# A long convolution in front of a recurrence: class sums and the skip product on GpSimd, inverses of 16 matmuls, later masks, and another way for the kernel values through DRAM

## The chip, the core and the metric

The kernel runs on one core of one Trainium2 chip. The core has five engines: TensorE (PE in the profile, with its weight loads as PEld), VectorE (DVE), ScalarE (ACT), GpSimd (POOL) and SyncE (SP). They share an on-chip memory of 128 partitions (SBUF); results of matmuls land in PSUM. Transfers run on 16 DMA engines and are issued from the queues of SP, ACT and POOL. The metric is the device time of one execution in microseconds, as the median of several runs of the same program.

## What is computed

Two independent parts are computed and concatenated along the last axis, for one batch of 2048 rows:

```python
# A: recurrent attention over segments of 32 rows, with 8 memory rows
for s in range(64):
    h = concat(mem, x[32*s : 32*s+32])            # 40 rows of 1024
    q, k, v = h @ Wq, h @ Wk, h @ Wv              # 32 heads of 128
    o = softmax(mask(q @ k.T / sqrt(128))) @ v
    o = o @ Wo                                    # 1024 wide
    mem = o[:8];  outs.append(o[8:])
# B: a long convolution, for each of 1024 columns d
K[d, l] = real(sum_n C[d,n] * exp(dt[d] * A[d,n] * l) * dt[d] * B[d,n])     # N = 128
y[l, d] = sum_{m <= l} K[d, l-m] * u[m, d]  +  u[l, d] * Dskip[d]
```

The reference does the convolution by FFT of length 4096. All inputs and the output are bf16.

## The kernel before

**Stage one** (0 to about 395 us of the profile) makes tables for part B, projections of those rows of part A that need no memory, and the kernel values K at chosen places. It is a list of steps in an order written out by hand (`ORDER`, L690), gone through 16 times (L1339). One transform of u into the frequency domain runs in it as a side job; its results, for four groups of 256 columns (`dq`) and four blocks of frequencies (`kc`), go to DRAM as `Ud` (L1011). GpSimd makes sums and differences there (L1007 to L1010, in `classes`). The values of K come out in two halves of 512 columns each, in tiles `KxT`. In `put_values` (L1072) the first half is written from SBUF into a DRAM buffer `Kd` with 44 small DMAs, each put into a list `late` that gives up one entry at each exponential (L1276). The second half is written whole as `Kx1` (L1075).

**Stage two** (about 395 to 632 us) has 16 passes, b = 0 to 15, one for each pair (dq, kc). A pass does the following.

- PE makes the spectrum of K for the next pass, `spectrum(b + 1, ...)` (L1238): 40 matmuls of 128x256 into tiles `hps` (before pass 4 `pa`), from values `ks` in SBUF.
- DVE multiplies it by the transform of u (`times_u`, L1394, four operations, one input in PSUM and one in SBUF), then turns (`rotate`, L1397 and L1398, both inputs in SBUF), then makes the sum and the difference of two halves (L1469, both inputs in SBUF) into a bf16 tile `Bt`.
- SP loads the next pass's `Ud` block (`load_u`, L1229), and weights of part A into places that have come free (`next(resident)`, L266).
- From b = 4 on, PE does two inverses (`products_back`, L1519): 32 matmuls of 128x256 each, from `Bt` of the dq before and the matrices `MI`. ACT makes negated copies of parts of `MI` for them (L1485) and writes the result as bf16 (`yb`, L1534). In the next pass DVE multiplies a loaded piece `uu` of u by `Dsk` (L1539) and adds `yb` (L1540), ACT issues the output DMA.

After pass 15 eight inverses are left, three of them begun with the first three blocks (`inverse_begin`); between them SP issues twelve weight loads and then one at a time (L1620).

Beside that, at b = 2 GpSimd multiplies four rows of values by four rows of u (L1596), and behind it in its queue, at b = 4, stand the identity and the masks of part A (`constants`, L222: 36 operations at L235 and some more). The second half's values are put in order by `load_second` (L1091): 12 small DMAs a pass from DRAM to SBUF (L1102) or to DRAM (L1105) at b = 3 to 6, and one load at the end (L1108). `spectrum(8, ...)`, which PE runs in pass 7, is the first to use them.

**Stage three** (632 us to the end) is part A: 64 segments one after the other. In each, PE goes through all weights; most stay in SBUF, twelve blocks of 512 KB are loaded again in each segment through four slots `wst` (L334). The first segment also loads the last weights of Wo (`W_o`, L266).

All queues are filled in program order (`manual_schedule`): what stands behind a waiting instruction on its engine waits too.

Of the kernel before, what the change touches and what calls it, by code (L numbers as in the profile page):

```python
# [221 lines left out]
def constants(tc, ahead):  # L222
# [4 lines left out]
    make_identity(nc, ident[:])  # L227
    nc.gpsimd.memset(mask[:], 0.0)
# [18 lines left out]
    ahead.consts = ident, mask, BD, BDx, BDL, hT  # L247
    return hT
# [454 lines left out]
def part_b(ctx, tc, u, A_re, A_im, B_re, B_im, C_re, C_im, log_dt, Dskip, out_b, ahead, copies, residents, first_state):  # L703
# [12 lines left out]
    Kd = dram.tile([641, DH], BF16, name="Kd")  # L716
    Kx1 = dram.tile([128, NF * 128], BF16, name="Kx1")
    Kd1 = dram.tile([256, DH], BF16, name="Kd1")
# [340 lines left out]
    def part_out(sb, h, kp):  # L1059
# [4 lines left out]
        if sb % 8 == 7 and h == 1:  # L1064
            put_values(sb)

    late = []

    PLACED = ((0, 0, ((8, 1, 32),)), (8, 256, ((8, 2, 16),)), (16, 384, ((4, 1, 4), (8, 4, 8), (40, 1, 4))),
              (24, 512, ((0, 1, 4), (4, 2, 2), (8, 8, 4), (40, 2, 2), (44, 1, 4))))  # L1070

    def put_values(sb):  # L1072
        kx = KxT["t"]
        if sb // 8:
            late.append(lambda: sy.dma_start(out=Kx1[:], in_=kx[:].rearrange("p j c -> p (j c)")))  # L1075
            return

        def put(out, in_):
            late.append(lambda: sy.dma_start(out=out, in_=in_))
        for g in range(4):  # L1080
            dsl = slice(128 * g, 128 * g + 128)
            for p0, u0, cols in PLACED:
                n_j = sum(n for _, _, n in cols)
                dst = Kd[u0:u0 + 8 * n_j, dsl].rearrange("(i j) d -> i j d", j=n_j)
                at = 0
                for j0, js, n in cols:
                    put(dst[:, at:at + n], kx[32 * g + p0:32 * g + p0 + 8, j0:j0 + js * (n - 1) + 1:js, :])
                    at += n
            put(Kd[640:641, dsl], kx[32 * g + 31:32 * g + 32, NF - 1, :])

    def load_second(KT):  # L1091
        rows = Kx1[:].rearrange("p (j c) -> p j c", j=NF)
        for g in range(4):
            for p0, u0, cols in PLACED:
                n_j = sum(n for _, _, n in cols)
                at, p = 0, 32 * g + p0
                for j0, js, n in cols:
                    src_ = rows[p:p + 8, j0:j0 + js * (n - 1) + 1:js, :]
                    if len(cols) == 1:
                        for lo in range(0, 8 * n_j, 128):  # L1100
                            o = DH * ((u0 + lo) // 128) + 128 * g
                            sy.dma_start(out=KT[:, o:o + 128], in_=src_[lo // n_j:(lo + 128) // n_j])  # L1102
                            yield
                    else:
                        sy.dma_start(out=Kd1[u0 - 384:u0 - 384 + 8 * n_j, 128 * g:128 * g + 128].rearrange("(i j) d -> i j d", j=n_j)[:, at:at + n], in_=src_)  # L1105
                        yield
                    at += n
        sy.dma_start(out=KT[:, 3 * DH:5 * DH].rearrange("p (j d) -> p j d", j=2), in_=Kd1[:].rearrange("(j p) d -> p j d", p=128))  # L1108

    def load_k(KT, lo):  # L1110
        n_ = KT.shape[1] // DH
        sy.dma_start(out=KT.rearrange("p (j d) -> p j d", j=n_), in_=Kd[128 * lo:128 * (lo + n_), :].rearrange("(j p) d -> p j d", p=128))
        return [KT[:, DH * j:DH * j + DH] for j in range(n_)]
# [664 lines left out]
```

## Time and profile before

| | |
|---|---|
| median of 3 runs | 1980.21 us (1974.15 to 1983.52) |
| the profiled execution | 1981.69 us, its span 1979.9 us |
| mean granted TensorE clock | 0.977 |
| PE busy | 1840.5 us (93%) |
| DVE busy | 1371.1 us (69%) |
| ACT busy | 949.7 us (48%) |
| GpSimd (POOL) busy | 389.8 us (20%) |
| moved by DMA | 589.91 MB, mean 298 GB/s |

The profile's page gives busy times, a picture of the span in 40 slices, the DMA queues, and the chain of work that ended last. The trace behind it can be asked for groups of instructions by line, for the order of time on an engine, for waits, and for busy time in given stretches. A line such as L1394 is a line of the kernel. A row of a timeline has the start, the length (both in us), the engine, the line, the operation, what it writes and reads with its shape, and how many such instructions were merged; in brackets stands the engine's idle time ahead of it and what ended it. The tile names are the program's own.

### The profile page before, as it was taken

To read this page: it belongs to the slowest core of one execution; us is meant where nothing else is said; L and a number is where in the kernel's file an instruction comes from. 1 tells how busy PE (TensorE), PEld (TensorE's weight loads), DVE (VectorE), ACT (ScalarE), POOL (GpSimd) and SP (SyncE) were. 2 spreads that over 40 slices of the span, in tenths; PEclk is the share of its full clock that TensorE was granted. 3 is DMA by queue.
4 is the path that set the end of the run, shared out by engine and by line. 5 is a ranking of instruction groups with operands and counts; after the bars stand their busy time and mean duration, and the time that the engine had idled before them with its cause. 6 is when DMAs were issued, how large, how long until landed. Compare 5 with 4: busy or idle time off the path is not lost.

```text
span 1979.9 us, 74693 instructions
## 1 busy us (share of the span) xinstructions
PE 1840.5 (93%) x32006; PEld 1133.3 (57%) x32044; DVE 1371.1 (69%) x3401; ACT 949.7 (48%) x1678; POOL 389.8 (20%) x823
## 2 busy tenths in 40 slices
PE   8999999787998799999999999999999999999999
PEld 3666566456786455555555555555555555555554
DVE  8699999787893466666666666767666666666650
ACT  8799999832123344434444444444434343434330
POOL 2354454212000111111111111111111111111120
PEclk9999999779999799999999999999999999999999
DMA  7989888765478899999999999999999999999991
GB/s 221 255 238 265 264 239 251 210 223 185 144 250 298 312 338 336 351 333 339 340 338 333 348 347 345 350 339 349 340 336 341 337 344 338 344 342 348 328 344 37
DMA packets 329728, 589.91 MB, mean 298 GB/s; under 512 B 87812, under 2 KB 203368, under 8 KB 327220
## 3 DMA queue, kind: packets, MB, share of 16 engines
q1 hardware_dynamic: 277208, 530.64, 78.4%
q10 hardware_dynamic: 45532, 29.57, 4.9%
q0 software_dynamic: 6656, 24.92, 3.4%
q8 instruction: 251, 4.11, 0.9%
q14 instruction: 81, 0.66, 0.1%
HBM read 528.52 MB, written 67.26 MB: 301 GB/s over the span
## 4 chain that ended last, share of the span: by engine, by line
PE 40%; DMA 22%; DVE 3%; ACT 1%; issue 1%; POOL 0%; ACTq 0%; SPq 0%; POOLq 0%; DVEq 0%
PE acc L408 23%; DMA wst<-WD_o 8%; PE pp L521 8%; DMA wst<-WD_v 6%; DMA wst<-WD_k 3%; PE pe L658 3%; PE tr L419 2%; DMA arena<-PKd 2%; DMA wst<-WD_q 1%; DMA out_dram<-arena 1%; PE pv L489 1%; DVE arena L615 1%; PE pv L493 1%; PE sc L433 1%; ACT arena L615 1%
## 5 line engine op out<-in xcount | busy, mean ns | idle before, releaser
L408 PEld LDWEIGHTS <-a_hT 128*32 128x32 bf16 x12352 | 328.2, 96 | 308.8 <-issue 54.0
L414 ACT CAST arena<-acc 128x512 bf16<-128x512 f32 x384 | 225.1, 586 | 395.0 <-PE acc L408 317.6
L521 PEld LDWEIGHTS <-arena 128*32 128x32 bf16 x8256 | 217.0, 96 | 91.0 <-issue 66.4
L408 PE MATMUL acc<-wst,a_hT 128*32 128x512 bf16 x2304 | 229.4, 381 | 24.1 <-DMA wst<-WD_v 16.4
L422 POOL COPY arena<-arena 128x128 bf16<-128x128 bf16 x128 | 37.3, 292 | 842.5 <-DMA arena<-PKd 274.0
L329 DVE TENSOR_SCALAR arena<-keep 128x256 int32<-128x256 int32 (+1 forms) x512 | 175.7, 395 | 31.5 <-PE acc L408 29.1
L408 PE MATMUL acc<-XM,a_hT 128*32 128x512 bf16 x2560 | 185.9, 380 | 0.0
L521 PE MATMUL pp<-W_o,arena 128*32 128x256 bf16 x3584 | 122.6, 274 | 7.3 <-DMA W_o<-in_A_Wo_dram 7.3
L452 ACT ACTIVATE sc<-sc 128x160 f32<-128x160 f32 (+1 forms) x192 | 63.9, 333 | 126.0 <-DVE sc L449 125.5
L448 DVE TENSOR_REDUCE a_mx<-sc 128x4 f32<-128x160 f32 (+1 forms) x192 | 71.7, 373 | 75.0 <-PE sc L436 75.0
L197 PE MATMUL pro<-XM,wsl 128*128 128x512 bf16 x480 | 117.4, 382 | 5.9 <-DVE kst L206 2.2
L408 PE MATMUL acc<-W,a_hT 128*32 128x512 bf16 x1536 | 119.3, 382 | 0.2 <-issue 0.2
L536 DVE COPY arena<-tr 128x512 bf16<-128x512 bf16 x64 | 27.2, 425 | 126.2 <-PE tr L419 126.2
L456 DVE TENSOR_REDUCE a_mx<-sc 128x4 f32<-128x160 f32 (+1 forms) x192 | 72.9, 379 | 55.4 <-ACT sc L452 55.0
L1519 PE MATMUL yp<-Bt,MI 128*128 128x256 bf16 x680 | 105.2, 274 | 0.0
L408 PE MATMUL acc<-g,a_hT 128*32 128x512 bf16 x1024 | 102.2, 381 | 0.0
L1283 DVE TENSOR_SCALAR nr<-ptt 128x456 f32<-128x456 int16 x128 | 80.3, 628 | 29.8 <-PE ptt L1261 26.9
L483 POOL TENSOR_TENSOR arena<-arena,a_BD 128x128 bf16<-128x128 bf16 x128 | 51.0, 399 | 237.8 <-DVE arena L466 222.8
L615 ACT CAST arena<-pp 128x128 bf16<-128x128 f32 x64 | 17.0, 266 | 164.9 <-DVE arena L615 164.9
L1275 ACT ACTIVATE E<-pa 128x648 bf16<-128x648 f32 x128 | 87.8, 713 | 15.8 <-PE pa L1267 13.9
L521 PE MATMUL pp<-wst,arena 128*32 128x256 bf16 x1536 | 76.6, 275 | 19.3 <-DMA wst<-WD_o 17.4
L408 PE MATMUL acc<-wq,a_hT 128*32 128x512 bf16 x1024 | 91.2, 382 | 0.0
(333 smaller groups left out, 4024.4 us busy)
## 6 DMA issues: line engine op xcount, KB each, us to landing
wst<-WD_v SPq DMA_DIRECT2D x256, 512.0 KB
wst<-WD_k SPq DMA_DIRECT2D x192, 512.0 KB
wst<-WD_o SPq DMA_DIRECT2D x192, 512.0 KB
wst<-WD_q SPq DMA_DIRECT2D x128, 512.0 KB
Ud<-ux POOLq DMA_DIRECT2D x16, 1024.0 KB, 8.2
wq<-Ud SPq DMA_DIRECT2D x32, 512.0 KB
wsl<-in_A_Wk_dram SPq DMA_DIRECT2D x16, 512.0 KB
wsl<-in_A_Wv_dram SPq DMA_DIRECT2D x16, 512.0 KB
```

What stands on the lines that cost most here:

```text
L197: nc.tensor.matmul(a[:], lhsT=w[:, kc, 128 * j:128 * j + 128], rhs=xTl[:, kc, :, :].rearrange("p s k -> p (s k)"), start=(kc == 0), stop=( ...
L329: nc.vector.tensor_scalar(out=out.bitcast(I32), in0=in_.bitcast(I32), scalar1=0, scalar2=None, op0=ALU.bitwise_or)
L408: nc.tensor.matmul(a[32 * g:32 * g + 32, o_:o_ + rhs.shape[1]], lhsT=hT[:, kc, :], rhs=rhs, start=(kc == 0), stop=(kc == KC - 1), tile_pos ...
L414: nc.scalar.copy(out=q, in_=a[:])
L448: nc.vector.tensor_reduce(out=m_, in_=x, axis=AX.X, op=ALU.max)
L452: nc.scalar.activation(out=flat(sc, i), in_=flat(sc, i), func=ACT.Exp, scale=scale)
L456: nc.vector.tensor_reduce(out=m_, in_=x, axis=AX.X, op=ALU.add)
L521: nc.tensor.matmul(po[32 * qt:32 * qt + 32, o_:o_ + rhs.shape[1]], lhsT=oT[:, h % 4, (h % 16) // 4, :], rhs=rhs, start=False, stop=(h == 3 ...
L658: nc.tensor.matmul(pe[n][:], lhsT=left[2 * b + hi // 16][:, 128 * (hi % 16):128 * (hi % 16) + 128], rhs=wo[u][:, 1024 * hh + 512 * n:1024 ...
L1275: sc.activation(out=T["E", r, e // 4][:, lo:lo + 8 * NE].rearrange("p (i c) -> p i c", i=2), in_=T.pop(("p", r, e))[:, :, 0:4 * NE], func= ...
L1283: v.tensor_scalar(out=T["n", r, e // 4][:, lo:lo + 8 * NT], in0=T.pop(("t", r, e))[:, 0:8 * NT].bitcast(I16)[:, 0:16 * NT:2], scalar1=floa ...
L1519: pe.matmul(yp[:, b, :], lhsT=m_[:, b, cs, kc, :], rhs=Bt[:, kc, j, half, c_, :], start=(kc == 0 and cs == 0 and half == 0), stop=(kc == 3 ...
```

## The change

- The sum and the difference of the two halves (L1469) go to an f32 tile `halves_` (one buffer) instead of `Bt`. GpSimd then makes the second sums in four operations of 128x512, two of them with the order of cosine and sine parts turned round, and writes bf16 `Bt` with eight parts a block.
- An inverse therefore has 16 matmuls instead of 32, and no negated copies of `MI`.
- `Dsk` is multiplied once by PLEN/2 on GpSimd (in stage one, at f = 10). GpSimd multiplies each loaded `uu` by it right behind its load (`load_inverse`), and an identity matmul for each half of an inverse adds the product to PSUM. The two DVE operations L1539 and L1540 go; the output DMA reads `yb` itself. `uu` has 5 buffers instead of 7, `yb` 4 instead of 2.
- `constants` makes only the identity at b = 4; the masks follow behind the sixth of the last eight inverses.
- Each half of the kernel values is written whole to DRAM by four DMAs (`Kx`, 256 bytes a piece), eight DMAs from DRAM to DRAM put two of its five blocks in order (`Kp`), and five loads bring them to SBUF. For the first half that is in stage one; for the second the eight DMAs are issued four each at b = 3 and 4, the loads at b = 6.

The core of the diff:

```diff
 def constants(tc, ahead):
     make_identity(nc, ident[:])
+    ahead.consts = ident, mask, BD, BDx, BDL, hT
+    yield hT
     nc.gpsimd.memset(mask[:], 0.0)
 ...
     def put_values(sb):
-        kx = KxT["t"]
-        if sb // 8:
-            late.append(lambda: sy.dma_start(out=Kx1[:], in_=kx[:].rearrange("p j c -> p (j c)")))
-            return
+        kx, half = KxT["t"], sb // 8
         for g in range(4):
 ...
+            late.append(lambda g=g: sy.dma_start(out=Kx[half][:, :, g, :], in_=kx[32 * g:32 * g + 32, :, :]))
+        late.extend([lambda: None] * (16 if half == 0 else 0))
+        for p0, cols in PIECES:
+            at = 0
+            for j0, js, n in cols:
+                (late if half == 0 else second).append(lambda p0=p0, at=at, j0=j0, js=js, n=n: sy.dma_start(
+                    out=Kp[half][p0 - 16:p0 - 8, at:at + n, :],
+                    in_=Kx[half][p0:p0 + 8, j0:j0 + js * (n - 1) + 1:js].rearrange("i j g c -> i j (g c)")))
+                at += n
 ...
     for f in range(16):
+        if f == 10:
+            gp.tensor_scalar(out=Dsk[:], in0=Dsk[:], scalar1=float(PLEN / 2), scalar2=None, op0=ALU.mult)
 ...
     def pointwise(b, s_):
+        X = halves_
         for j, op in ((0, ALU.add), (1, ALU.subtract)):
-            v.tensor_tensor(out=Bt[:, kc, j], in0=Y[:, 0], in1=Y[:, 1], op=op)
+            v.tensor_tensor(out=X[:, j], in0=Y[:, 0], in1=Y[:, 1], op=op)
+        for r, op in ((0, ALU.add), (2, ALU.subtract)):
+            gp.tensor_tensor(out=Bt[:, kc, 2 * r:2 * r + 2], in0=X[:, 0, 0], in1=X[:, 0, 1], op=op)
+        gp.tensor_tensor(out=Bt[:, kc, 2:8:5], in0=X[:, 1, 0], in1=X[:, 1, 1, ::-1], op=ALU.add)
+        gp.tensor_tensor(out=Bt[:, kc, 3:7:3], in0=X[:, 1, 0, ::-1], in1=X[:, 1, 1], op=ALU.subtract)
 ...
-    NIV, UU = 3, 7
+    NIV, UU = 3, 5
     def load_inverse(dq, c):
         sy.dma_start(out=uu[:], in_=u_v[r][:, mc:mc + 2, d])
+        gp.tensor_tensor(out=uu[:], in0=uu[:], in1=Dsk[:, d].unsqueeze(1).to_broadcast([128, 2, DQ]), op=ALU.mult)
 ...
                 for cs in range(2):
-                    g_cs = cs if j == 0 else 1 - cs
-                    minus = neg is not None and neg[0] <= cs < neg[1]
-                    for half, m_, c_ in ((0, MI[c // 2], cs), (1, mn if minus else MI[c // 2], g_cs)):
-                        pe.matmul(yp[:, b, :], lhsT=m_[:, b, cs, kc, :], rhs=Bt[:, kc, j, half, c_, :], start=(kc == 0 and cs == 0 and half == 0),
-                                  stop=(kc == 3 and cs == 1 and half == 1), skip_group_check=True)
+                    pe.matmul(yp[:, b, :], lhsT=MI[c // 2][:, b, cs, kc, :], rhs=Bt[:, kc, 2 * r + cs, :], start=(b == 0 and kc == 0 and cs == 0),
+                              stop=False, skip_group_check=True)
+            if kcs[-1] == 3:
+                pe.matmul(yp[:, b, :], lhsT=ident[:], rhs=uu[:, b, :], start=False, stop=True, skip_group_check=True)
 ...
-        def ending():
-            v.tensor_tensor(out=uu[:], in0=uu[:], in1=Dsk[:, d].unsqueeze(1).to_broadcast([128, 2, DQ]), op=ALU.mult)
-            v.tensor_tensor(out=uu[:], in0=uu[:], in1=yb[:], op=ALU.add)
-            unsent.append(lambda: sc.dma_start(out=out_v[r][:, mc:mc + 2, d], in_=uu[:]))
+        unsent.append(lambda: sc.dma_start(out=out_v[r][:, mc:mc + 2, d], in_=yb[:]))
 ...
-        for _ in range(12 if 2 < b < 7 else 0):
-            next(second, None)
+        for _ in range(4 if b in (3, 4) else 0):
+            second.pop(0)()
+        if b == 6:
+            ks.append(load_k(1, k1[:, 0:2560], 0))
 ...
     for n_ in range(8):
         inverses(1)
-        end()
+        if n_ == 5:
+            next(state)
```

More of the change, by code (lines that the diff above doesn't have):

```diff
@@ L715, in part_b @@
     Ud = dram.tile([4, 4, 128, 4, 2, DQ], F32, name="Ud")
-    Kd = dram.tile([641, DH], BF16, name="Kd")
-    Kx1 = dram.tile([128, NF * 128], BF16, name="Kx1")
-    Kd1 = dram.tile([256, DH], BF16, name="Kd1")
+    Kx = [dram.tile([32, NF, 4, 128], BF16, name="Kx%d" % i) for i in range(2)]
+    Kp = [dram.tile([16, 16, DH], BF16, name="Kp%d" % i) for i in range(2)]
     MId = dram.tile([16, 128, 2, 4, 128], BF16, name="MId")
@@ L1091, in load_second @@
[L1091 to L1108, printed above, removed]
@@ new lines, in put_values, with load_k @@
+        for p0, cols in PIECES:
[5 more added lines that the diff above has]
+                at += n
+    def load_k(half, KT, lo):
+        n_ = KT.shape[1] // DH
+        ks_ = [KT[:, DH * j:DH * j + DH] for j in range(n_)]
+        for j, t_ in enumerate(ks_):
+            c = lo + j
+            src_ = Kp[half][8 * (c - 3):8 * (c - 2)] if c > 2 else Kx[half][4 * c:4 * c + 4, 8:40] if c < 2 else Kx[half][8:16, 8:40:2]
+            sy.dma_start(out=t_, in_=src_ if c > 2 else src_.rearrange("i j g c -> i j (g c)"))
+        return ks_
@@ L1493, in inverses @@
             dq, c = todo.pop(0)
-            if not ready:
-                ready.append(negated(c))
-            inverse(dq, c, nxt.pop(0), *ready.pop(0))
+            inverse(dq, c, nxt.pop(0))
             if len(todo) >= NIV:
@@ L1728, in first_state @@
         nc = tc.nc
-        hT = constants(tc, ahead)
+        consts = constants(tc, ahead)
+        hT = next(consts)
         nc.sync.dma_start(out=xt[:].rearrange("p k r -> p (k r)"), in_=ahead.VXd[0, :, 256:])
```

72 lines of the change are left out of this document (19 added, 53 removed).

## The prediction, made before the changed kernel was run

> **What bounds the kernel now.** I read the busy time by stage first. The rows have the stretch, its length, the busy time of PE, PEld, DVE, ACT and POOL with instruction counts, the granted clock, the busy share of the DMA engines, and GB/s.
>
> ```profile
> 395.00:453.00 58.00, 49.60 (x399) 33.31 (x388) 49.32 (x46) 17.61 (x36) 14.19 (x35) 0.77 0.62 215
> 453.00:518.00 65.00, 48.53 (x397) 40.21 (x395) 43.38 (x49) 11.71 (x13) 4.27 (x17) 0.87 0.58 183
> 518.00:600.00 82.00, 82.00 (x744) 71.41 (x743) 74.89 (x86) 24.39 (x27) 0.00 (x0) 1.00 0.63 196
> 600.00:672.00 72.00, 55.84 (x667) 38.10 (x665) 22.95 (x63) 21.42 (x31) 2.80 (x8) 0.90 0.94 326
> 672.00:1979.00 1307.00, 1238.72 (x25523) 715.23 (x25524) 833.29 (x2594) 519.59 (x1141) 205.53 (x513) 1.00 0.92 329
> ```
>
> The change leaves stage three (the last row) alone, and adds to stage one only work beside its matmuls. So the passes and the stretch behind them count. From 518 us PE is busy without a gap, DVE is close behind, GpSimd does nothing, and the DMA engines have a third free. From 600 us DMA is at 0.94. Between 453 and 518 us nothing is full: something waits. In the order of time, DVE:
>
> ```profile
> 429.92 2.36 DVE L1469 TENSOR_TENSOR Bt<-y 128x1024 bf16<-128x1024 f32 x2
> ...
> 451.04 2.36 DVE L1469 TENSOR_TENSOR Bt<-y 128x1024 bf16<-128x1024 f32 x2
> ...
> 515.74 2.36 DVE L1469 TENSOR_TENSOR Bt<-y 128x1024 bf16<-128x1024 f32 x2
> ...
> 565.08 1.22 DVE L1394 TENSOR_TENSOR z<-wq,hps 128x1024 f32<-128x1024 f32 x1
> 566.21 1.22 DVE L1394 TENSOR_TENSOR y<-wq,hps 128x1024 f32<-128x1024 f32 x1
> ...
> 569.60 0.42 DVE L1539 TENSOR_TENSOR uu<-uu,Dsk 128x512 bf16<-128x512 bf16 x1
> ...
> 571.67 0.42 DVE L1540 TENSOR_TENSOR uu<-uu,yb 128x512 bf16<-128x512 bf16 x1 [0.73 <-ACT yb L1534]
> 572.01 1.22 DVE L1397 TENSOR_TENSOR y<-y,z 128x1024 f32<-128x1024 f32 x1
> 573.15 1.22 DVE L1398 TENSOR_TENSOR y<-y,z 128x1024 f32<-128x1024 f32 x1
> 574.40 2.36 DVE L1469 TENSOR_TENSOR Bt<-y 128x1024 bf16<-128x1024 f32 x2
> ...
> 597.75 2.36 DVE L1469 TENSOR_TENSOR Bt<-y 128x1024 bf16<-128x1024 f32 x2
> ```
>
> The sums L1469 mark the ends of passes 2, 4, 8, 13 and 15. Passes 14 and 15 took (597.75 - 574.40) / 2 = 11.68 us each, but 5 to 8 took (515.74 - 451.04) / 4 = 16.2 us each: four passes lost 18 us. The whole stretch from 4 to 15 took 146.7 us. An operation of 128x1024 takes a slot of 1.13 us (565.08 to 566.21). The matmuls of a steady pass:
>
> ```profile
> 516.41 6.71 PE L1519 MATMUL yp<-Bt,MI 128*128 128x256 bf16 x60
> ...
> 523.71 4.53 PE L1238 MATMUL hps<-k,XM 128*128 128x256 bf16 x40
> 528.08 0.27 PE L1519 MATMUL yp<-Bt,MI 128*128 128x256 bf16 x1
> ```
>
> At 4.37 us for 40 (523.71 to 528.08, 0.109 us each) a pass is 40 + 64 matmuls and two small ones, 11.6 us: **PE sets the pass**. What slowed passes 5 to 8 is in the waits between 400 and 640 us and in SP's order:
>
> ```profile
> DVE z L1394 <- DMA wq<-Ud: 17.2, 4, 6.0
> PE hps L1238 <- DMA k<-Kd: 11.7, 1, 11.7
> ```
>
> ```profile
> 444.89 7.06 SPq L1105 DMA_DIRECT2D Kd<-Kx  x8
> ...
> 552.69 0.89 SPq L1477 DMA_DIRECT2D uu<-in_B_u_dram  x2
> ```
>
> Twelve small DMAs a pass cost SP some 0.9 us each, over 10 us, and the next `Ud` block stands behind them.
>
> **The change, part by part.**
>
> *Work that goes from PE and DVE.* An inverse has 16 + 2 matmuls instead of 32: 28 x 0.109 = 3.1 us a pass, and PE needs 8.5 us. DVE loses two pairs L1539 and L1540 and keeps eight slots, 9.1 us. The negated copies on ACT (24 us busy of 82) are off the path: nothing.
>
> *Work that GpSimd gets.* Its nearest rows:
>
> ```profile
> 26.96 3.18 POOL L916 TENSOR_TENSOR part<-x,part 128x1024 bf16<-128x1024 f32 x1 [13.63 <-ACT part L906]
> 35.25 2.13 POOL L916 TENSOR_TENSOR part<-x,part 128x1024 bf16<-128x1024 f32 x1 [5.11 <-ACT part L906]
> ...
> 136.90 1.27 POOL L1007 TENSOR_TENSOR ux<-us 128x512 f32<-128x512 f32 x1 [2.23 <-DVE us L1036]
> 138.14 1.27 POOL L1008 TENSOR_TENSOR ux<-us 128x512 f32<-128x512 f32 x1
> 139.37 2.78 POOL L1010 TENSOR_TENSOR ux<-us 128x256 f32<-128x256 f32 x4
> ...
> 437.35 2.11 POOL L1596 TENSOR_TENSOR k<-g,k 4x1024 bf16<-4x1024 bf16 x1 [64.52 <-DMA k<-in_B_u_dram]
> 440.82 1.01 POOL masks.py:199 TENSOR_SCALAR_AFFINE_SELECT a_ident<-a_ident 128x128 bf16<-128x128 bf16 x1
> 442.02 13.78 POOL L235 TENSOR_SCALAR_AFFINE_SELECT a_mask<-a_mask 32x24 bf16<-32x24 bf16 x36
> ```
>
> ```profile
> L483 POOL TENSOR_TENSOR arena<-arena,a_BDL 128x128 bf16<-128x128 bf16 x128 | 51.4, 401 | 0.0
> L886 POOL TENSOR_TENSOR x<-natAr,dtb 128x1024 f32<-128x1024 bf16 x1 | 1.9, 1892 | 6.3 <-DMA natAr<-in_B_A_re_dram 6.3
> ```
>
> A class sum of 128x512 f32: 1.24 us (136.90 to 138.14). Bounds: half of the shorter L916, 1.06, and half of the longer, 1.59. The product u times D, 128x512 bf16 with one operand repeated: half of L1596, 1.05, half of L886, 0.95, or four times L483, 1.6. I take 1.1, near the two that have long rows. A pass gives GpSimd 4 x 1.24 + 2 x 1.1 = 7.1 us. Alone this would fit beside DVE's 9.1.
>
> *But the two engines exclude each other.* On DVE, beside the GpSimd rows at 26.96 and 437.35:
>
> ```profile
> 26.94 1.22 DVE L892 SCALAR_TENSOR_TENSOR x<-y,y 128x1024 f32<-128x1024 f32 x1
> ...
> 436.51 1.22 DVE L1394 TENSOR_TENSOR y<-wq,pa 128x1024 f32<-128x1024 f32 x1
> 437.76 2.78 DVE L1397 TENSOR_TENSOR y<-y,z 128x1024 f32<-128x1024 f32 x1
> ```
>
> L1397 has two SBUF inputs; it took 2.78 instead of 1.22 us, and ended 1.1 us after the GpSimd product (437.35 + 2.11 = 439.46). L1394, one input in PSUM, overlapped the same product and kept its 1.22 us. On the other side, the first L916 began behind L892, which has two SBUF inputs, and was 1.05 us longer than the second. So of DVE's eight slots the last four (L1397, L1398, two L1469) cannot run beside GpSimd, the four L1394 can. A pass then is 4.94 (class sums, beside 4 x 1.13 of L1394) + 4 x 1.13 + 2 x 1.1 = 11.7 us; behind the product L1397 needed 1.08 us instead of 1.22, so at a pass's three turns from GpSimd to DVE I take 0.3 off: **11.4 us, about what PE's 11.68 is now**. The bound has changed, and the steady pass hardly gains. PE has room: even at the first row's clock of 0.77 it would need 8.5 / 0.77 = 11.0 us. Bounds, all rows low or high: 10.2 (0.2 more for hand-overs) and 4.54 + 5.2 (two sums in two pieces of 0.69, as L1010) + 3.2 = 13.0.
>
> The Trainium skill says this too (SBUF — State Buffer, section "SBUF: two separate sides"): a DVE operation with two SBUF inputs and a GpSimd operation that reads SBUF take one port pair in turns, each for its whole length. That rule speaks against moving the sums; the trace agrees, with 2.78 against 1.22 us. It has no gain at the hand-over and would give 11.7 us a pass and 1965 us in the end. The skill's GPSIMD Engine Reference (3.1 Elementwise) gives 2.6 cycles an element at 1.2 GHz, by which a 128x512 operation is an estimated 1.1 us, the class sum too: 0.5 us less a pass and about 1956 us in the end.
>
> *The second half's values.* The 48 small DMAs become four at b = 3, four at b = 4 and five at b = 6. At 0.9 us each SP is held 3.6 to 4.5 us in these passes, less than the 6.7 us (four slots, two products) between the last L1394 of a pass, which frees the `Ud` tile, and the first of the next. The 17.2 and 11.7 us of waits go, and passes 5 to 8 run at the steady length: 11 passes at 11.4, and 1.2 us for the identity between them, 126.6 instead of 146.7: **20.1 us gained** (bounds 33 and 3).
>
> *b = 2 to 4.* In GpSimd's queue stand the class sums of pass 2, L1596 with three small followers (437.35 to 440.82, 3.4 us), three products (3.3), and only then the class sums of pass 3, which pass 4's sums on DVE need (one buffer). From the end of pass 2 (432.3) these are 4.9 + 3.4 + 3.3 + 4.9 us, with four turns of DVE for pass 3 between them (4.5) and three to four for pass 4 behind (4.0): 25.0 us to the end of pass 4, against 453.4 - 432.3 = 21.1 now. **4 us lost** (bounds 3 and 6). If a row piece or a `uu` lands late, GpSimd waits at the head of its queue, the sums behind it, then DVE. From b = 4 on there is room: pass 11 ends at 576.8 - 2 x 11.68 = 553.4, its `uu` loads are issued at 552.69, and 4.9 us of class sums stand ahead of their products.
>
> *The four dumps in place of `Kx1`, the 12 DMAs in place of 44 in stage one, `Dsk` times a constant.* Nothing: the first half's blocks are wanted only in the last of stage one's sixteen rounds, some five rounds after they are written; the second half's dumps stand on SP ahead of pass 2's `Ud` block, where DMA is at 0.62 and GpSimd busy 14 of 58 us. Without that cover up to 5 us, one block late by a dump or two.
>
> *The tail and the masks.* The chain that ended last has:
>
> ```profile
> 652.67 6.94 DMA W_o<-in_A_Wo_dram
> ...
> 659.67 11.44 DMA wst<-WD_o
> ```
>
> Behind pass 15 the eight inverses need half the matmuls, some 12 us less. But DMA is at 0.94 there, the last `uu` loads stand behind twelve weight loads, and weights set the end of the first segment. PE cannot pass them. I take **3 us gained** (bounds 6 gained, 2 lost). The masks (13.8 us) now run behind the last products, while segment one starts; the scores that want them stand in the middle of a segment of 1307 / 63 = 20.7 us, so they may be 3 us late, in front of the longer waits for weights: nothing. If no such wait is left, 3 us.
>
> **The sum**: -20.1 + 4 - 3 = -19.1. The profiled execution took 1981.7 us (1979.9 span, 1.8 around it), 1.5 above the median, 1980.2. From the one 1962.6, from the other 1961.1: **1962 us**.
>
> **The rivals.**
> - *The engines run side by side*: then DVE's 9.2 us bound the pass: 11 x 9.2 = 101, 45.5 gained, with the tail and nothing lost at b = 3 about 49: 1932 us. For it: L1394 was not slowed. Against: L1397 was. 8%.
> - *GpSimd is dearer, and the passes get longer*: with 1.59 a sum and 1.6 a product a pass is 4.54 + 6.36 + 3.2 = 14.1, eleven 155 + 1: 9.6 lost instead of 20.1 gained, 7 at b = 3, 1 gained behind: 1997 us. It decides from a pass of 13.1 us, that is 8.6 to 8.9 of GpSimd's time. For it: the turned order and the repeated operand stand in no f32 row. Against: L1007, L1008. 13%.
> - *The passes gain, the end does not*: if transfers alone set the first segment's end, only the tail changes: 1979 us. For it 0.94 of DMA from 600 us. Against: these loads wait for places that the passes free, and at 518 to 600 us a third is free. 9%.
>
> **How the numbers follow.** The forecast has 70%; its own range is 1946 to 1985 by the bounds of its terms. It takes in the third rival and leaves out the first and the second, 21%, of which the second's lower end lies within; so the range is 1946 to 1985. Half a per cent (10 us) is about what a measurement can tell from no change. Of the forecast's 70% I give 62 to faster by more than that, 7 to within, 1 to slower; the first rival is faster, the second slower, the third within: faster 0.70, same 0.16, slower 0.14.
>
> **What would show it.** Steps: L1394 and L1238 wait no more for `Ud` and values between 453 and 518 us; passes of 11.4 us with PE no longer full; L1397, L1398 and the sums stretched to 2 us or more wherever GpSimd works, L1394 not; class sums at 1.24, products at 1.1; the first segment's wait for `WD_o` still there. Wrong if DVE keeps 1.22 us throughout (first rival) or GpSimd's operations alone are over 1.5 us (second).

## The result

The changed kernel takes 1965.28 us (median of 13 runs, 1962.06 to 1978.45); beside it on the same chip the kernel before took 1979.36 us (13 runs). The ratio is 0.9949, with a 95% interval of 0.9924 to 0.9974. The profiled execution took 1964.7 us (span 1962.9), 17.0 less than the one before. The forecast was 1962.

In the busy time by stage (the columns are those of the table of before) PE is no longer full in the passes, and the slow stretch from 453 us is gone:

```profile
453.00:518.00 65.00, 54.03 (x453) 44.24 (x451) 64.17 (x46) 7.16 (x12) 58.23 (x37) 0.92 0.67 212
518.00:590.00 72.00, 58.24 (x468) 46.87 (x467) 65.79 (x49) 7.76 (x13) 65.91 (x42) 0.91 0.75 231
```

DVE and GpSimd (the third and the fifth busy time) are both busy for nine tenths or more from 453 to 590 us. How they share a pass stands in the order of time, first DVE, then GpSimd. The line numbers are those of the changed kernel: L1374 is the multiplication (before L1394), L1377 and L1378 the rotation, L1451 the pair of half sums (before L1469), L1453 to L1455 the class sums, L1465 the product of u and D.

```profile
457.67 3.24 DVE L1451 TENSOR_TENSOR hv<-y 128x1024 f32<-128x1024 f32 x2
...
514.00 3.12 DVE L1451 TENSOR_TENSOR hv<-y 128x1024 f32<-128x1024 f32 x2
...
562.11 1.21 DVE L1374 TENSOR_TENSOR z<-wq,hps 128x1024 f32<-128x1024 f32 x1
...
565.50 1.21 DVE L1374 TENSOR_TENSOR y<-wq,hps 128x1024 f32<-128x1024 f32 x1
...
568.01 2.17 DVE L1378 TENSOR_TENSOR y<-y,z 128x1024 f32<-128x1024 f32 x1
570.28 3.12 DVE L1451 TENSOR_TENSOR hv<-y 128x1024 f32<-128x1024 f32 x2
...
581.50 3.12 DVE L1451 TENSOR_TENSOR hv<-y 128x1024 f32<-128x1024 f32 x2
```

```profile
561.13 3.41 POOL L1453 TENSOR_TENSOR Bt<-hv 128x512 bf16<-128x512 f32 x2 [1.16 <-DVE hv L1451]
...
565.74 1.27 POOL L1455 TENSOR_TENSOR Bt<-hv 128x512 bf16<-128x512 f32 x1
566.97 4.22 POOL L1465 TENSOR_TENSOR uu<-uu,Dsk 128x512 bf16<-128x512 bf16 x2
```

From pass 9 to pass 15 a pass took (581.50 - 514.00) / 6 = 11.25 us on average (single ones 10.4 to 12.2), against a forecast of 11.4. The four L1374 ran beside the class sums and kept 1.21 us. L1378, with two SBUF inputs, began beside the first product and took 2.17; the pair L1451 took 3.12 in place of 2.36. From pass 4 to 15 it is 123.8 us (457.67 to 581.50) in place of 146.7.

The first segment still ends with the wait for a weight, and its first transposition of a new state (`tro`, the first sign of a finished segment, here "the first state") came 16.6 us earlier; pieces of the chain of work, first of the kernel before, then of the changed one:

```profile
672.63 0.59 PE tro L621 x2
```

```profile
642.77 11.74 DMA wst<-WD_o
...
656.02 0.58 PE tro L622 x2
```

The 17.0 us by stretches of the two profiled executions, against the forecast's terms:

| stretch | forecast | measured |
|---|---|---|
| up to the sums of pass 0 (402.4, now 406.2) | 0 | +3.8 |
| sums of pass 0 to those of pass 4 (48.6, now 51.5) | +4 | +2.9 |
| pass 4 to pass 15 (146.7, now 123.8) | -20.1 | -22.9 |
| the pair of sums of pass 15 (2.4, now 3.1) | 0 | +0.7 |
| its end to the first state (72.5, now 71.4) | -3 | -1.1 |
| first state to the end (1307.3, now 1306.9) | 0 | -0.4 |
| sum | -19.1 | -17.0 |

### The profile page after: what moved, and what is told of

The parts are those of the page before. It is cut to its first block, busy times and chain, and to the rows that moved or that the text cites. A ratio compares the mean times of both kernels' runs of the same rounds, so it can differ in the third digit from the quotient of the medians.

```text
span 1962.9 us, 73759 instructions
## 1 busy us (share of the span) xinstructions
PE 1799.1 (92%) x31558; PEld 1089.2 (55%) x31596; DVE 1370.2 (70%) x3337; ACT 918.9 (47%) x1654; POOL 543.4 (28%) x920
## 4 chain that ended last, share of the span: by engine, by line
PE 45%; DMA 28%; DVE 18%; ACT 6%; issue 4%; POOL 0%; SPq 0%; ACTq 0%; DVEq 0%; POOLq 0%
PE acc L409 22%; DMA wst<-WD_v 9%; DMA wst<-WD_o 9%; PE pp L522 8%; DMA wst<-WD_k 3%; PE pe L659 3%; DMA wst<-WD_q 2%; PE tr L420 2%; DMA arena<-PKd 2%; PE pro L184 2%; DVE nr L1261 2%; DVE y L1374 1%; DVE hv L1451 1%; PE pa L1216 1%; DVE y L1378 1%
## 5 line engine op out<-in xcount | busy, mean ns | idle before, releaser
L409 PE MATMUL acc<-W,a_hT 128*32 128x512 bf16 x1536 | 119.2, 381 | 0.0
L1504 ACT ACTIVATE yb<-yp 128x512 bf16<-128x512 f32 x29 | 17.3, 597 | 157.9 <-PE yp L1492 146.4
L522 PE MATMUL pp<-wst,arena 128*32 128x256 bf16 x1536 | 76.5, 275 | 15.4 <-DMA wst<-WD_o 13.1
```

The costliest lines, as they stand in the source:

```text
L409: nc.tensor.matmul(a[32 * g:32 * g + 32, o_:o_ + rhs.shape[1]], lhsT=hT[:, kc, :], rhs=rhs, start=(kc == 0), stop=(kc == KC - 1), tile_pos ...
L522: nc.tensor.matmul(po[32 * qt:32 * qt + 32, o_:o_ + rhs.shape[1]], lhsT=oT[:, h % 4, (h % 16) // 4, :], rhs=rhs, start=False, stop=(h == 3 ...
```

## The experiments

The theory is the prediction's: SP's queue of small DMAs held passes 5 to 8, which is where the gain lies; elsewhere PE's bound gave way to one as long, DVE and GpSimd taking turns. The rivals: the gain came with the halved matmuls and the work on GpSimd; or a pass is bound by something else (PE's lower clock, GpSimd's whole time).

Times of one kernel spread over 10 us and more, so mechanisms are read from stretches of the profiles: from the pair of sums in pass 4 to that in pass 15, and from the end of the latter to the first state. Each stretch is that of one execution. Ratios are to the kernel before on the same chip, with 95% intervals; the runs used several chips, so medians of different rows are compared through the ratios.

| kernel | median us | ratio | pass 4 to 15 | 15 to first state |
|---|---|---|---|---|
| before | 1979.4 | 1 | 146.7 | 72.5 |
| changed | 1965.3 | 0.9949 [0.9924, 0.9974] | 123.8 | 71.4 |
| values_alone | 1962.8 | 0.9941 [0.9918, 0.9963] | 126.9 | 69.5 |
| sums_alone | 1976.7 | 1.0002 [0.9976, 1.0029] | 140.0 | 70.0 |
| product_dve | 1960.4 | 0.9932 [0.9910, 0.9954] | 122.7 | 69.9 |
| dsk_late | 1966.8 | 0.9968 [0.9944, 0.9991] | 124.9 | 72.8 |
| no_class_sums | 1947.4 | 0.9844 [0.9809, 0.9879] | 115.8 | 74.5 |
| masks_early | 1975.2 | 0.9991 [0.9971, 1.0011] | 132.7 | 72.2 |
| tail_loads_first | 1977.5 | 1.0010 [0.9990, 1.0029] | 125.5 | 76.5 |
| turns_fewer | 1960.0 | 0.9913 [0.9881, 0.9945] | 119.3 | 71.2 |
| stores_at_once | 1968.5 | 0.9963 [0.9944, 0.9981] | 125.4 | 72.6 |
| turns_fewer_2 | 1953.0 | 0.9886 [0.9857, 0.9916] | 119.2 | 69.8 |
| stores_by_gpsimd | 1978.5 | 1.0008 [0.9989, 1.0028] | 122.1 | 85.1 |
| dumps_spread | 1965.4 | 0.9942 [0.9917, 0.9967] | 126.8 | 71.1 |

### The two halves of the change, each alone

`values_alone` is the kernel before with the new `put_values`, `load_k` and `second` alone:

```diff
-    Kd = ...; Kx1 = ...; Kd1 = ...
+    Kx = [dram.tile([32, NF, 4, 128], BF16, ...) for i in range(2)]
+    Kp = [dram.tile([16, 16, DH], BF16, ...) for i in range(2)]
...
-        for _ in range(12 if 2 < b < 7 else 0):
-            next(second, None)
+        for _ in range(4 if b in (3, 4) else 0):
+            second.pop(0)()
+        if b == 6:
+            ks.append(load_k(1, k1[:, 0:2560], 0))
```

> The kernel before with the new way of the kernel values alone (four dumps a half, pieces, block loads); sums, inverses, products and masks as before. Theory (SP's queue of small DMAs held passes 5 to 8, PE sets all others): passes 5 to 8 fall from 16.2 to 11.7 us each, the stretch from pass 4 to pass 15 from 146.7 to about 130 us, and the time falls by 16 to 17 us, to about 1963: nearly the whole gain of the change. If the dumps also cost the first stage something, its rounds 9 and 10 (18.7 us each in the kernel before) get longer here. Rival (the gain came with the sums, products and half the matmuls): the time stays above 1974 and passes 5 to 8 stay above 14 us.

`sums_alone` is the changed kernel with these hunks undone.

> The changed kernel with the kernel values moved the old way (44 small stores, one dump of the second half, 48 small loads in passes 3 to 6); sums, inverses of 16, products on GpSimd, identity and late masks stay. Theory: passes 5 to 8 wait for SP again, some 16 us each; the seven other passes are 0.5 us shorter than PE's 11.7, 3.4 us gained in all, against 3.6 us lost at passes 2 to 4 and 3 us in the first stage: 1978 to 1984 us, no faster than before. Rival (the gain came with this part): 1970 us or less.

DVE's pairs of sums, first in `values_alone` (passes 4, 8 and 15), then in `sums_alone` (pass 8; there the pair of pass 4 began at 456.92); below them DVE's wait for `Ud`, first in `values_alone` between 453 and 518 us, then in `sums_alone` between 453 and 530 us:

```profile
455.79 2.36 DVE L1446 TENSOR_TENSOR Bt<-y 128x1024 bf16<-128x1024 f32 x2
...
500.78 2.36 DVE L1446 TENSOR_TENSOR Bt<-y 128x1024 bf16<-128x1024 f32 x2
...
582.65 2.36 DVE L1446 TENSOR_TENSOR Bt<-y 128x1024 bf16<-128x1024 f32 x2
```

```profile
518.89 2.36 DVE L1474 TENSOR_TENSOR hv<-y 128x1024 f32<-128x1024 f32 x2
```

```profile
DVE z L1371 <- DMA wq<-Ud: 0.8, 1, 0.8
```

```profile
DVE z L1397 <- DMA wq<-Ud: 19.4, 4, 7.3
```

With the values alone passes 5 to 8 take 11.2 us each; with the sums alone (518.89 - 456.92) / 4 = 15.5, and the wait for `Ud` is as long as in the kernel before. The one half carries the whole gain, the other none: the theory holds, the first rival falls. By the medians `values_alone` gained 10.6 us on its chip (1962.8 against 1973.4), less than the 16 to 17 expected. The sums alone do shorten the stretch from pass 4 to 15 by 6.7 us, but passes 0 to 4 took 3.4 us longer in that trace and began 2.5 us later, and the time did not move.

### What makes a steady pass

`product_dve` gives the products back to DVE; the identity matmul stays.

```diff
-        gp.tensor_tensor(out=uu[:], in0=uu[:], in1=Dsk[:, d]..., op=ALU.mult)
+        unmade.append(lambda: v.tensor_tensor(out=uu[:], in0=uu[:], in1=Dsk[:, d]..., op=ALU.mult))
...
         next(points)
+        products()          # runs what stands in unmade; also ahead of each last inverse
```

> The changed kernel with the products of u and D on DVE, as in the kernel before (0.42 us each), instead of on GpSimd; the identity matmul still adds them. Theory of turns (a pass is the class sums beside the four L1374, then the four DVE operations with two SBUF inputs and the products, one at a time): a pass is 4.94 + 4.53 + 2 x 0.42 - 0.2 = 10.1 us instead of 11.2; 12 us less in eleven passes, 2 to 3 us less at passes 2 to 4 and behind the last: 1949 to 1952 us. Rival 1 (PE at the lower granted clock, or the single buffer of the half sums, sets the pass): passes stay at 11.2 us and the time within 3 us of the changed kernel. Rival 2 (weights set the end): passes fall to 10.1, the time does not.

DVE in one pass of it, and GpSimd beside it:

```profile
506.38 2.36 DVE L1451 TENSOR_TENSOR hv<-y 128x1024 f32<-128x1024 f32 x2
...
513.19 1.01 DVE L1469 TENSOR_TENSOR uu<-uu,Dsk 128x512 bf16<-128x512 bf16 x2
514.12 1.21 DVE L1377 TENSOR_TENSOR y<-y,z 128x1024 f32<-128x1024 f32 x1
...
516.57 1.23 DVE L1451 TENSOR_TENSOR hv<-y 128x1024 f32<-128x1024 f32 x1
```

```profile
507.75 3.36 POOL L1453 TENSOR_TENSOR Bt<-hv 128x512 bf16<-128x512 f32 x2 [4.36 <-DVE hv L1451]
...
512.29 1.28 POOL L1455 TENSOR_TENSOR Bt<-hv 128x512 bf16<-128x512 f32 x1
```

DVE has more to do than in the changed kernel, and yet the pass is 516.57 - 506.38 = 10.2 us, as expected (10.1): nothing is stretched any more but the products themselves, which begin before the last class sum ends. The time is not shown to be below that of the changed kernel (the intervals overlap; 1949 to 1952 us was expected), since passes 5 and 7 took 14.8 and 13.9 us. In both DVE stood before a product whose `uu` was late on SP, in pass 7 behind the five loads of values, in pass 5 behind four pieces, of whose 10.05 us 7.4 were a wait for a store of ACT (more on that below):

```profile
468.55 0.43 DVE L1469 TENSOR_TENSOR uu<-uu,Dsk 128x512 bf16<-128x512 bf16 x1 [4.35 <-DMA uu<-in_B_u_dram]
```

```profile
455.24 10.05 SPq L1079 DMA_DIRECT2D Kp<-Kx  x4
```

`no_class_sums` leaves the class sums out; DVE's pair writes what the matmuls read.

```diff
-            v.tensor_tensor(out=X[:, j], in0=Y[:, 0], in1=Y[:, 1], op=op)
-        for r, op in ...: gp.tensor_tensor(out=Bt[...], ...)
-        ...
+            v.tensor_tensor(out=Bt[:, kc, 4 * j:4 * j + 4]..., in0=Y[:, 0], in1=Y[:, 1], op=op)
```

> The changed kernel without the class sums: DVE's pair writes what the matmuls read, and GpSimd keeps the products alone (what the matmuls read is then not the class sums). Theory of turns (the class sums run beside the four L1374 and cost nothing; the four DVE operations with two SBUF inputs and the two products go one at a time): a pass is 4.53 + 4.53 + 2.2 - 0.2 = 11.0 to 11.1 us against 11.2 with the class sums, though GpSimd has 4.9 us less to do; a few us are gained at passes 2 to 4. Rival (GpSimd's whole time, or the loop through the one buffer of half sums, makes the pass): a pass falls to DVE's 9.1 to 9.3 us and pass 15 ends 20 us earlier.

Passes of 9.3 to 11.3 us came out from pass 8 on. GpSimd's products, then DVE, in one of the shortest and in the longest:

```profile
517.49 2.27 POOL L1460 TENSOR_TENSOR uu<-uu,Dsk 128x512 bf16<-128x512 bf16 x2 [7.96 <-PE hps L1216]
...
554.16 4.24 POOL L1460 TENSOR_TENSOR uu<-uu,Dsk 128x512 bf16<-128x512 bf16 x2 [6.99 <-DMA uu<-in_B_u_dram]
561.04 3.25 POOL L1460 TENSOR_TENSOR uu<-uu,Dsk 128x512 bf16<-128x512 bf16 x2 [2.63 <-DMA uu<-in_B_u_dram]
```

```profile
514.35 2.36 DVE L1450 TENSOR_TENSOR Bt<-y 128x1024 bf16<-128x1024 f32 x2
...
523.67 2.36 DVE L1450 TENSOR_TENSOR Bt<-y 128x1024 bf16<-128x1024 f32 x2
...
554.07 3.31 DVE L1450 TENSOR_TENSOR Bt<-y 128x1024 bf16<-128x1024 f32 x2
...
563.19 2.17 DVE L1378 TENSOR_TENSOR y<-y,z 128x1024 f32<-128x1024 f32 x1
565.40 2.36 DVE L1450 TENSOR_TENSOR Bt<-y 128x1024 bf16<-128x1024 f32 x2
```

Where the products fell beside the four L1374 (517.49), the pass took 523.67 - 514.35 = 9.3 us. The pass of 565.40 - 554.07 = 11.3 us has four products: two beside its pair of sums (554.16; the pair took 3.31 in place of 2.36) and two beside the rotation (561.04; L1378 took 2.17 in place of 1.22). These two operations, each 0.95 us longer, are nearly the whole difference. My number was wrong: I had the products always behind the L1374, but with no class sums ahead of them most start when their `uu` lands. The rival's number came out only where the products met nothing but L1374. What decides is which DVE operation a GpSimd operation meets.

### Where the masks stand

```diff
         hT = next(consts)
+        next(consts)                 # the masks at b = 4 again
...
-        if n_ == 5:
-            next(state)
```

> The changed kernel with the masks built in pass 4 again, as in the kernel before, instead of behind the sixth of the last eight inverses. Theory: the 13.8 us stand in GpSimd's queue between pass 4's class sums and its products; GpSimd has only 4 us to spare in a pass, so passes 5 and 6 lose 8 to 11 us together and pass 15 ends that much later: 1973 to 1976 us. Behind pass 15 nothing is gained. Rival 1 (they fit beside passes 4 to 6): passes as in the changed kernel, 1965 us. Rival 2 (the masks now hold the first segment): its end comes 3 us or more earlier behind pass 15 than in the changed kernel.

In `masks_early` GpSimd's queue, then DVE:

```profile
469.44 12.72 POOL L237 TENSOR_SCALAR_AFFINE_SELECT a_mask<-a_mask 32x24 bf16<-32x24 bf16 x36
...
485.56 2.48 POOL L1453 TENSOR_TENSOR Bt<-hv 128x512 bf16<-128x512 f32 x2
```

```profile
488.08 2.27 DVE L1451 TENSOR_TENSOR hv<-y 128x1024 f32<-128x1024 f32 x1 [8.32 <-POOL Bt L1453]
```

The class sums stood behind the masks, and DVE waited 8.3 us for them. Pass 4 to 15 is 8.9 us longer than in the changed kernel, the stretch behind it no shorter. So moving the masks is what keeps the work on GpSimd from costing 9 us, and late masks hold nobody.

### Stage one

`dsk_late` multiplies `Dsk` by the constant on ACT ahead of the passes:

```diff
-        if f == 10:
-            gp.tensor_scalar(out=Dsk[:], in0=Dsk[:], scalar1=float(PLEN / 2), ...)
...
+    sc.activation(out=Dsk[:], in_=Dsk[:], func=ACT.Copy, scale=float(PLEN / 2))
     for b in range(16):
```

> The changed kernel with D times the constant on ACT ahead of the passes instead of on GpSimd in round 10 of the first stage. Theory (this multiply took 4.34 us on GpSimd, ahead of the loads L752 in its queue, and held the first stage by 3 us): rounds 9 and 10 take 18.7 to 18.9 us again, not 19.5 and 21.0, and the passes begin 3 us earlier: about 1962 us. Rival (the dumps on SP hold the round): rounds and time as in the changed kernel, 1965 us.

`dumps_spread` puts seven empty places behind each of the first half's dumps (`late.extend([lambda: None] * 7)`) in place of sixteen behind all four.

> The changed kernel with seven empty places between the four dumps of the first half, so that other transfers of the first stage stand between them in SP's queue. Round 10 of the first stage took 21.0 us in every kernel with dumps and 18.7 in those without. Theory (four dumps of 1568 pieces of 256 bytes close together hold SP's queue, and ACT's cast behind it): round 10 falls to 18.7 to 19.6 us and pass 0 begins 2 us earlier; the time is 1961 to 1965 us, a change too small to be measured by time alone. Rival (the wait goes with a place in memory that the new order brings, not with SP): round 10 stays at 21.0 us or the loss moves to the next rounds.

The rounds are read from DVE's casts L1063, one row at the beginning of each of rounds 9 and 10 and of the next: the kernel before, the changed one, `dsk_late`, `dumps_spread`.

```profile
251.80 0.56 DVE L1063 CAST KxT<-kp 128x392 bf16<-128x392 f32 x1
...
270.53 0.56 DVE L1063 CAST KxT<-kp 128x392 bf16<-128x392 f32 x1
...
289.28 0.55 DVE L1063 CAST KxT<-kp 128x392 bf16<-128x392 f32 x1
```

```profile
251.96 0.56 DVE L1063 CAST KxT<-kp 128x392 bf16<-128x392 f32 x1
...
271.53 0.55 DVE L1063 CAST KxT<-kp 128x392 bf16<-128x392 f32 x1
278.08 0.57 DVE L1063 CAST KxT<-kp 128x392 bf16<-128x392 f32 x1 [2.26 <-PE kp L1055]
292.51 0.55 DVE L1063 CAST KxT<-kp 128x392 bf16<-128x392 f32 x1
```

```profile
251.75 0.56 DVE L1063 CAST KxT<-kp 128x392 bf16<-128x392 f32 x1
...
270.48 0.55 DVE L1063 CAST KxT<-kp 128x392 bf16<-128x392 f32 x1
...
291.46 0.55 DVE L1063 CAST KxT<-kp 128x392 bf16<-128x392 f32 x1
```

```profile
276.81 0.56 DVE L1063 CAST KxT<-kp 128x392 bf16<-128x392 f32 x1
...
295.56 0.55 DVE L1063 CAST KxT<-kp 128x392 bf16<-128x392 f32 x1
```

Before: 18.7 and 18.7 us. Changed: 19.6 and 21.0. Without the multiply on GpSimd round 9 is 270.48 - 251.75 = 18.7, round 10 stays at 21.0: my theory priced the multiply at 3 us, and it is 0.8; the time of `dsk_late` is not shown to differ from the changed kernel's. It is lost in one operation of DVE with two SBUF inputs, the second behind the multiply's beginning; first the changed kernel, then `dsk_late`:

```profile
259.61 1.40 DVE L1228 TENSOR_TENSOR gi<-E,wn 128x768 bf16<-128x768 bf16 x1
```

```profile
259.40 0.56 DVE L1228 TENSOR_TENSOR gi<-E,wn 128x768 bf16<-128x768 bf16 x1
```

So it is the turns again, not the loads that stand behind the multiply in GpSimd's queue. Over all fourteen kernels round 9 is 19.6 us in the eight with the multiply on GpSimd and 18.7 to 18.8 in the six without.

With the dumps spread round 10 is 18.75: the dumps, close together, are the other 2.2, through a wait of PE for a cast of ACT (behind it the 2.26 us above). Round 10 is 21.0 to 22.8 us in the eleven kernels with the dumps close together and 18.75 in the three others. But the theory of this run, a held queue of SP and a late cast behind it, falls: in all fourteen that cast begins 5.18 us behind the round's first cast L1063. What differs is that in the eleven the matmul `kp` waits for ACT, and in the three the same matmul has no wait and runs 2.2 us earlier. That is nearer to the rival; which place or order in the built program brings the wait is open.

`dumps_spread` is no faster than the changed kernel. Its first cast L1063 stood at 104.9 us against 99.65, so its passes began later (408.2 against 406.2 us) and not 2 us earlier as expected; from that cast to pass 0 it took 303.3 us against 306.5. And it lost 4.3 us in pass 5 (14.8 us): there the second of pass 4's sums waited for class sums, and the products met both operations of the rotation (2.16 and 2.17 us).

### Behind pass 15

```diff
-    NIV, UU = 3, 5
+    NIV, UU = 3, 7               # and two places for yb instead of four
...
+    nxt.extend(load_inverse(*todo[n_]) for n_ in range(NIV, 7))
     for n_ in range(8):
```

> The changed kernel with the next four loads of u for the last inverses issued ahead of the twelve weight loads that now stand before them (seven places for u instead of five, two for yb instead of four). Theory (weights set the end of the first segment): the wait of 13 us for u in GpSimd's queue goes, the inverses end some 10 us earlier, but from the end of pass 15 to the first state of the segments it still takes 70 to 72 us, and the time is within 3 us of the changed kernel. Rival (the last inverses hold the end): that stretch is 5 to 10 us shorter, and so is the time.

Two waits behind pass 15 in `tail_loads_first`, of ACT and of SP ahead of weight loads:

```profile
ACT yb L1504 <- DMA out_dram<-yb: 36.0, 10, 8.0
```

```profile
SPq L267 <- DMA out_dram<-yb: 17.4, 4, 7.7
```

The stretch got 5 us longer, which neither side expected. The inverses did not end earlier, since with two places for `yb` ACT waited 36 us for its stores; SP's weight loads waited 17.4 us for stores too, and in this run's chain of work there is hardly anything but stores of `yb` from 587 to 635 us. The run changed two things, and the second covered the first: what sets the end in the changed kernel is not settled by it. What `values_alone` shows is firmer: with all 32 matmuls an inverse the stretch is 69.5 us, so no gain of the halved matmuls shows there.

### A version with fewer turns

`turns_fewer` has the products on DVE between the rotation and the pair of sums, six places for u and three for `yb`, the pieces and blocks behind the loads of u, and the constant on ACT.

> The changed kernel with the products of u and D on DVE between the rotation and the pair of half sums, six places for u, the pieces and the loads of the second half's values behind the loads of u and a pass earlier, and D times the constant on ACT. Theory: passes of 10.2 us without the three stops that the first kernel with products on DVE had (4.6, 3.7 and 1.3 us, each behind a load of u or of values), 113 to 116 us from pass 4 to pass 15 instead of 123.7; pass 15 ends at 571 to 575 us instead of 584.6, and the time is 1951 to 1955 us. Rival (another wait takes their place, PE's clock or a load): pass 15 ends after 579 us.

Passes 8 to 15 took 10.0 to 10.2 us each, but passes 3, 6 and 7 took 16.7, 13.2 and 15.8, and pass 15 ended at 583.7 us, as the rival had it. A wait of SP that stands behind passes 6 and 7:

```profile
SPq L1467 <- DMA out_dram<-yb: 9.7, 1, 9.7
```

SP waited 9.7 us for a *store* of ACT before it issued a *load* of u. In the built program the DMAs of SP and ACT take eight completion counters in turn, and an issue waits for the DMA before it on its counter; ACT issues a store only behind its next copy. (This store had been issued at 471.89, and SP's load went out at 482.27: the wait was the store's own way to DRAM.) So I issued the stores at once, first alone:

```diff
-        while unsent:
-            unsent.pop(0)()
-        unsent.append(lambda: sc.dma_start(out=out_v[r][:, mc:mc + 2, d], in_=yb[:]))
+        sc.dma_start(out=out_v[r][:, mc:mc + 2, d], in_=yb[:])
```

> The changed kernel with each store of yb issued right behind its own copy on ACT instead of behind the next one. In the changed kernel SP waited some 29 us between 400 and 680 us for stores (out_dram<-yb), since the DMAs of SP and ACT take eight counters in turn and an issue waits for the DMA before it on its counter. Theory (turns set the passes, weights the rest): those waits of SP shrink to under 10 us, the steady pass stays at 11.2 us, pass 15 ends at most 2 us earlier, and from the end of pass 15 to the first state it takes 3 to 6 us less than 71.4, since the twelve weight loads no longer wait for stores: 1959 to 1963 us. Rival (the stores' waits are hidden): all stretches and the time within 2 us of the changed kernel.

Nothing is gained: both stretches stay within 2 us, as the rival had it. SP still waited for stores, 8.6 us in one wait in the passes and 6.2 in two behind them. In the first, ACT issued the store at 456.67, and the piece behind it on SP followed at 463.76: some 7 us of the wait are again the store's way to DRAM, which an earlier issue does not shorten.

`turns_fewer_2` is `turns_fewer` with this edit, the first loads of u two passes earlier, and two loads in place of eight for the last row.

> The kernel turns_fewer with the stores issued at once, the first three loads of u in pass 1 instead of pass 3, and the last row of the values by two loads to four partitions instead of eight. Theory: turns_fewer lost 6.2, 3.0 and 5.6 us in passes 3, 6 and 7, where DVE waited for u or for the blocks of u's spectrum and SP for a store's counter; without these the passes take 10.0 us from the third on, 111 to 113 us from pass 4 to pass 15, pass 15 ends at 568 to 573 us, and the time is 1946 to 1951 us. Rival (another load is late in those passes, or what is gained is given back behind pass 15): 1957 us or more.

It is the fastest kernel with the whole computation, 0.9886 [0.9857, 0.9916], below the changed one's interval. Passes from 8 on take 10.0 to 10.1 us, but passes 5 to 7 still 12.3, 14.1 and 12.7, so the number expected was not reached. The last try moved the stores to GpSimd's queue, which takes other counters:

```diff
-        sc.dma_start(out=out_v[r][:, mc:mc + 2, d], in_=yb[:])
+        unsent.append(lambda: gp.dma_start(out=out_v[r][:, mc:mc + 2, d], in_=yb[:]))
```

> The kernel turns_fewer_2 with the stores of yb issued by GpSimd behind its class sums of the next pass (five places for u, four for yb). Theory: the stops left in passes 5 to 7 of turns_fewer_2 (2.3, 4.1 and 2.7 us beyond 10.0) come from SP, which waited 15 us there and behind for the counters of stores; stores of GpSimd take other counters, the stops go, passes 4 to 15 take 110 to 113 us instead of 119.2, pass 15 ends at 570 to 574 us, and the time is 4 to 8 us below that of turns_fewer_2 (1953). Rival (SP's own thirteen loads of the second half's values hold those passes, or GpSimd's two issues a pass, some 0.6 us each, lengthen them): pass 15 ends after 577 us.

In `stores_by_gpsimd`, a wait between 440 and 590 us, and one row of DVE:

```profile
POOL out_dram L1510 <- issue: 37.2, 10, 5.7
```

```profile
551.24 4.76 DVE L1375 TENSOR_TENSOR y<-y,z 128x1024 f32<-128x1024 f32 x1
```

Passes 5 to 7 did become 10.1, 10.4 and 11.4 us, which fits that most of the stops there came from the stores' counters, though it also has a place less for u and one more for `yb`. But each store then held GpSimd's queue, the class sums behind it came late, DVE had to wait a turn of 4.76 us, passes 13 to 15 took 12.1 to 13.4 us, pass 15 ended at 584.2 us (the rival's side), and the stretch behind it grew to 85 us. The Trainium skill (SBUF — State Buffer, section "SBUF: two separate sides") says that while DVE runs an operation in a 2-port mode, GpSimd is locked out of the shared ports and cannot write the descriptors of a DMA issued from its queue. The 37 us of waits before L1510, for which the profile shows no cause ("issue"), would fit that, but no run here tells it from other reasons.

## Why the prediction was right, and where not

- **What bounds the kernel** was read rightly: four passes lost to SP's queue. `values_alone` and `sums_alone` show it from both sides. Of the signs, DVE's wait for `Ud` is gone; PE still waited for values, 7.2 us in three waits, and passes 5 to 8 took 11.3 us each all the same.
- **SP's price** was too low in one pass: "At 0.9 us each SP is held 3.6 to 4.5 us", but the four pieces at b = 4 held it 8.9 us, of which 6.2 were a wait for a store of ACT on a shared counter. The prediction had no such wait. Here it cost nothing (pass 5 took 10.5 us); in `product_dve`, where the wait was 7.4 us, pass 5 took 14.8.
- **The steady pass**: 11.4 forecast, 11.25 measured, with the makeup that the prediction gave (L1374 beside the class sums, the rest in turns). `product_dve` and `no_class_sums` show that the turns make it. (The lower bound of 10.2 comes out at 10.4 by its own terms, since the four L1394, 4.5 us, last longer than four class sums at 1.06.) "The steady pass hardly gains" is the reason why half of the change is worth nothing.
- **The rows for GpSimd**: class sums 1.27 us (1.24 taken), products 1.15 alone (1.1 taken; the 4.22 for two includes DVE's turns). The Trainium skill's GPSIMD Engine Reference (3.1 Elementwise), by which both were an estimated 1.1, is below the class sum that the trace shows.
- **Passes 2 to 4**: 4 us forecast, 2.9 measured to the pair of pass 4 and 0.9 in that pair itself (3.24 in place of 2.36).
- **Stage one** is the step that failed: "Nothing: the first half's blocks are wanted only in the last of stage one's sixteen rounds". It asked who waits for what the dumps write. It did not apply its own rule, that GpSimd and a DVE operation with two SBUF inputs exclude each other, to the multiply, in a stage where DVE and ACT are busy for 93 to 95 of 100 us. The two rounds cost 3.1 us: 0.8 the multiply, shown in the one DVE operation that it stretched, and 2.2 a wait of PE that comes with the dumps close together and that nobody had foreseen. Of the other 0.7 us of the 3.8 nothing can be said: six kernels with the same first stage reached pass 0 305.1 to 307.9 us behind their first cast.
- **Tail and masks**: 3 us forecast, 1.1 measured (71.4 against 72.5), which is no shown gain: two kernels with the same code there took 71.1 and 72.8. That late masks cost nothing was right.
- **The rivals**: "side by side" falls with L1378 at 2.17 us, "GpSimd is dearer" with 1.27 and 1.15, "the end does not gain" with the first state 16.6 us earlier.

The sum came out 2.1 us low: 2.8 more gained in passes 4 to 15 than forecast and 1.1 less lost in passes 0 to 4 stand against 3.8 in stage one, 0.7 in the last pair and 1.9 missing in the tail; 0.4 came with the segments. So the mechanism was right where the gain lies, but that the sum came within 2.1 us is in part luck, since errors of up to 3.8 us cancelled.

Open: why dumps close together make PE wait for that cast of ACT, what sets the end behind pass 15, and why a store of `yb` is under way for 7 to 10 us.

## What to carry to other kernels

When a change both relieves a queue and moves work between engines, price the two apart: here thirteen larger DMAs in place of 48 small ones were the whole gain, and the moved work was a new bound as long as the old one. Here work went to GpSimd for nothing only beside DVE operations with an input in PSUM (1.21 us beside it, as alone); a short product (0.42 us on DVE, 1.15 and a turn on GpSimd) made the steady pass shorter on DVE (10.2 against 11.25 us). Of every step that is moved into a nearly full stage, ask what it runs beside and what its issue waits for, not only who reads its result.

## What was not expected of the hardware

- GpSimd's `Dsk` times a constant, 128x1024 bf16 with one input, took 4.34 us in stage one, twice the 2.11 of the 4x1024 product with the same number of elements a partition. Beside it DVE's L1228 took 1.40 us in place of 0.56; whether DVE's turns or the operation itself make the 4.34 was not tried.
- The 36 small mask operations took 12.72 us beside DVE's passes and 8.21 us behind them, while DVE's rotation beside them kept 1.22 to 1.23 us: here it was GpSimd that waited.
- What stands behind the first state, 62 more states and the end, no kernel here changes; it took 1306.9 us in the changed kernel, 1297.0 in `dsk_late` and 1310.9 in `turns_fewer_2`: one execution doesn't tell a gain of a few us, a stretch of its trace does.
